# One core, three layers fused: weight conversions split into held steps, and key features and spatial-weight conversions held behind expert work

## The chip, the core and the metric

One core of a Trainium2 chip runs the whole program. Its engines each work through a list of instructions in a fixed order: TensorE does matmuls (PE in the profile, PEld for the loading of its weights), VectorE (DVE), ScalarE (ACT) and GpSimd (POOL) work element by element, and SyncE (SP) issues the DMAs. An engine waits at an instruction until the semaphores that it needs are set, and everything behind it on that engine waits too. The metric is the device time of one execution in microseconds.

## The reference

For a batch of 4 and a sequence of 1088, in single precision:

```
attention  a = S1 k, b = S2 k;  k_p = outer(a, b) per head (64 features);  q_p the same from q
           kv = sum_s k_p v;  z = sum_s k_p;  x = (q_p kv) / (q_p z + 1e-6)
experts    xk = mu_k x + (1 - mu_k) x_prev;  xr = mu_r x + (1 - mu_r) x_prev
           x = sigmoid(xr w_r) * (relu(xk w_k)^2 w_v)            128 -> 1024 -> 128
gMLP       h = relu(x w_in);  u, v = halves of h (512 each);  v_n = v normalised over its 512
           v_s = w_spatial v_n + b_spatial;  out = (u * v_s) w_out     w_spatial: 1088 x 1088
```

## The kernel before, in words

A matmul operand is split into a high part H and a rest L, both in a rounded format, and a product is three matmuls (`mm3`, L126: H by H, H by L, L by H). So every weight and every activation is converted first: a copy into H (`copy`, L129, on ACT) and a subtraction that leaves L (`low`, L132, on DVE or POOL).

The weights of the layers w_k, w_v, w_r, w_in and w_out arrive in 64-bit form. `split64` turns one block of 512 columns into H and L by integer work: on DVE L139, L141, L142, L143 and L144, on ACT L140, L146 and the copy into H, on POOL the product L147. The late ones, two blocks of w_in and one of w_out, are called `conv_late`. The spatial weight arrives in single precision, in 27 tiles (k, c): 9 blocks of rows k, of which the last (k = 8) holds the 64 rows of the tail and the bias, by 3 chunks c of 384, 384 and 320 columns. `wload` fetches a tile into one of two raw buffers (`st`), `wconv` converts it, and `wstep` does both, one tile behind the other. Raw tiles of both kinds go through one list, `pending_raw`, first in, first out.

The time up to some 210 us is one loop over g = 0 to 99. Step g issues the up-projection of one of 96 expert blocks (`up`: matmuls `p<-m,k`, a relu on ACT at L355, a square on POOL at L358 or on DVE at L363), the split of the square (`sqsplit`, L375 or L387 and L132) and the down-projection four steps behind (`down`: `p<-w,xs1H`, `p<-w,wvT`, then the gating on DVE at L403). A table of planned steps (`plan(g, fn)`) adds at each g what else is due:

- `q_feat`, `q_turn`, `q_num`, `q_out` for the next chunk of queries: matmuls L203, features on DVE or POOL (L214, tile `n1L`), transposes L255, products L272, a division on DVE (L276 to L278), and a transpose back, L290, copied to `x`.
- `prep`: on POOL the difference of neighbours (L312, `m<-x`), on DVE the mix (L313, `mx`), then H on ACT and L on DVE (tile `m`): the moving operand of 8 steps of `up`. `prep_r` does the same for the gate (L329, tiles `xrH` and `xrL`, the latter by POOL).
- `k_feat` for batches 2 and 3: three chunks each of key features, into `n0H`, `n0L` and `n1H`. Each is 6 matmuls (L203), a copy on ACT and one product of 768 columns (L214) on DVE, except `n0H` of batch 2 and `n0L` of batch 3, which POOL makes. They are needed by `k_sum`, some steps later.
- `x_tile` and `v_tile` of batch 0 (the v half of h): `p<-winL,w`, `p<-winH,w`.
- the conversions above, and from g = 93 on the first spatial products (`spatial`): `p<-w,n0H` and `p<-w,n0L` for d = 0, `p<-w,n1H` and `p<-w,n1L` for d = 1, each over 8 blocks k, and the tail (L561, L562, tile `T`). After the loop those of d = 2 (`p<-w,m`) and d = 3 (`p<-w,k`) follow.

The order of instructions on each engine isn't the order of this code. A scheduler goes over the traced program with an estimate of times and puts next on an engine what it takes to be ready first, so that an instruction whose operands are early can land far ahead of work that the code issues before it. What limits this is `behind(anchors, fn)`: an instruction that `fn` issues gets an edge to the anchor on its own engine and is not placed ahead of it. `anchor` holds three instructions, the last ones of the expert work so far on DVE, ACT and POOL. `late(fn)` is `behind` with all three. Before the change, `conv_late` is held by the DVE anchor alone and as one piece; `wconv` by the DVE and ACT anchors, and only for chunk c = 0; `k_feat` by nothing.

Of the kernel before, what the change touches and what calls it, by code (L numbers as in the profile page):

```python
# [18 lines left out]
NF = DFF // 128  # L19
# [16 lines left out]
NFILL = 3  # L36
VP = 2 * (HD + 1)
G1 = 26
WS = 30
WR = 2.5  # L40
C0 = 17
CS = 6
# [37 lines left out]
def attn_moe_gmlp(ctx: ExitStack, tc: tile.TileContext, qT, kT, va, st, wk, wv, wr, win, wout,  # L80
# [10 lines left out]
    def sb(tag, shape, dt=F32):  # L91
        uid[0] += 1
        return pool.tile(shape, dt, tag=tag, bufs=1, name=f"{tag}_{uid[0]}")
# [7 lines left out]
    def rot(*tags):  # L101
        i = count.get(tags, 0)
        count[tags] = i + 1
        return tags[i % len(tags)]
# [23 lines left out]
    def copy(dst, src):  # L128
        return SE.activation(out=dst, in_=src, func=AF.Copy)  # L129
# [1 line left out]
    def low(eng, L, src, H):  # L131
        return eng.tensor_tensor(out=L, in0=src, in1=H.bitcast(F32), op=ALU.subtract)  # L132

    def split64(raw, n, H, L, total=None):
        hi, lo = raw[:, :, 1], raw[:, :, 0]
        x = rot(*CVT)
        th, s = sb(f"w{x + 1}", [128, 2, n], I32), sb(f"w{x + 2}", [128, n], I32)
        t, h = th[:, 0], th[:, 1]
        VE.tensor_scalar(out=t, in0=hi, scalar1=0x7FFFFFFF, scalar2=9, op0=ALU.bitwise_and, op1=ALU.logical_shift_right)  # L139
        SE.activation(out=h, in_=t, func=AF.Relu, scale=4096.0, bias=ebias)  # L140
        VE.tensor_scalar(out=s, in0=hi, scalar1=0x1FF, scalar2=15, op0=ALU.bitwise_and, op1=ALU.logical_shift_left)  # L141
        VE.scalar_tensor_tensor(out=s, in0=lo, scalar=17, in1=s, op0=ALU.logical_shift_right, op1=ALU.bitwise_or)  # L142
        VE.scalar_tensor_tensor(out=h, in0=hi, scalar=-0x80000000, in1=h, op0=ALU.bitwise_and, op1=ALU.bitwise_or)  # L143
        VE.tensor_scalar(out=t, in0=h, scalar1=-0x800000, scalar2=None, op0=ALU.bitwise_and)  # L144
        if total is None and n in CONVP:
            SE.activation(out=s.bitcast(F32), in_=s, func=AF.Copy, scale=2.0 ** -35)  # L146
            GE.tensor_tensor(out=L, in0=s.bitcast(F32), in1=t.bitcast(F32), op=ALU.mult)  # L147
        else:
            VE.scalar_tensor_tensor(out=L, in0=s, scalar=2.0 ** -35, in1=t.bitcast(F32), op0=ALU.mult, op1=ALU.mult)
        if total is None:  # L150
            copy(H, h.bitcast(F32))
        else:
            VE.tensor_tensor(out=total, in0=h.bitcast(F32), in1=L, op=ALU.add)

    def flat(r):
        return r.rearrange("p a b -> p (a b)")

    pending_raw = []
# [6 lines left out]
    def conv64():  # L165
        split64(*pending_raw.pop(0))
# [131 lines left out]
    anchor, prep_L = [None, None, None], [None, None]  # L298
# [547 lines left out]
    SE.activation(out=warm, in_=half, func=AF.Sigmoid)  # L846
    Sl, Ss = sb(m(10), [128, 16]), sb(m(8), [128, 16])
    split64(rawS, 16, None, Sl, Ss)
    Sb = sb("Sbd", [128, 2 * NH, 16])
    VE.tensor_tensor(out=Sb, in0=Ss.unsqueeze(1).to_broadcast([128, 2 * NH, 16]),  # L850
# [13 lines left out]
    at = [-1]  # L864
# [3 lines left out]
    def wnext():  # L868
        if wi[0] < len(worder):
            k, c = worder[wi[0]]  # L870
            free = {t: QE[2 + (t > 1)] if t < 4 else GL + GW if t < 8 else C0 + 2 * CS + 1 for t in range(17)}
            if at[0] < max([free.get(t, 0) for t, _ in wplace(k, c)] + [W1G if c == 1 else NI * NF if c else 0]):
                return
            wload(k, c)
        wi[0] += 1

    def wstep():
        if pending_raw:
            behind([x for x in anchor[:2] if x is not None and pending_raw[0][1] == 0], wconv)
        wnext()  # L880

    load_q(0, (0,))
# [14 lines left out]
    def behind(anchors, fn, *a):  # L897
        with ExitStack() as es:
            for x in anchors:
                es.enter_context(tc.issue_after(x.ins))  # L900
            fn(*a)
# [31 lines left out]
    def plan(g, fn, *a):  # L933
        todo.setdefault(g, []).append(lambda: fn(*a))

    def gated(fn):
        return wraps(fn)(lambda *a: behind(prep_0, fn, *a))

    NI = B * NCH
    QS = [None, 0, 4] + [8 + QD * n for n in range(NI - 3)]  # L940
    QS[1:] = [x + y for x, y in zip(QS[1:], QJ[1:])]
    for j in range(1, NI):
        sp = 1 if j < 3 else 2
        for n, fn in enumerate((q_feat, q_turn, q_num, q_out)):
            plan(QS[j] + sp * n, gated(fn) if j < 3 and n == 0 else fn, j)
        e = QS[j] + 3 * sp
        plan(max(8 * j - 6, e + 1), prep, j)
        plan(max(8 * j - 4, e + 2), prep_r, j)
        plan(8 * j - 2, receive, j)
        plan(8 * j - 1, gate, j)  # L950
    QE = [QS[3 * b + 2] + 1 for b in range(B)]
    for b in range(1, B):
        last = QS[3 * b]
        ks = (3, 6, 8) if b == 1 else (last - 19, last - 12, last - 5)
        for c in range(NCH if b > 1 else 0):
            plan(ks[c], k_feat, b, c)
        if b > 1:
            plan(last + 1, k_sum, b, 0)
            plan(last + 2, k_sum, b, 1)
        if b + 1 < B:  # L960
            plan(last + 3, load_v, b + 1)
            plan(QE[b - 1], load_k, b + 1)
            plan(QE[b - 1], load_q, b + 1)
    def late(fn, *a):
        behind([x for x in anchor if x is not None], fn, *a)

    def conv_first():
        late(conv64)

# [1 line left out]
        H, L = [x.bitcast(F32).rearrange("p (f two d) -> p f two d", two=2, d=128)[:, 2 * h:2 * h + 2, 1] for x in (wvH, wvL)]  # L971
        GE.tensor_tensor(out=wvT[:, 2 * h:2 * h + 2], in0=H, in1=L, op=ALU.add)

    def conv_late():
        behind(anchor[:1], conv64)

    for n in range(2):
        plan(R0[n], total_wv, n)
# [3 lines left out]
    plan(R1 + 4, gate, 0)  # L982
    for n, x in enumerate(wseq[5:]):
        plan(C0 - 2 + CS * n, load64, *x)
        plan(C0 + CS * n, conv_late)
    for n in range(2):
        plan(WS - 2 + n, wnext)
    for n in range(NK + 1):
        plan(WS + int(WR * n), wstep)
    xv["v"] = sb("tt", [128, NT - HALF, DG])  # L990
    xv["x"] = sb("w17", [128, 4, 2, 128], F32R)
    for j in range(NT):
        plan(VS[j] - 1, late, x_tile, j)
        plan(VS[j], late, v_tile, 0, j)
        plan(VS[j] + 1, late, v_rest)
# [3 lines left out]
    for n in range(8):  # L999
        plan(GL + GW + n, wstep)  # L1000
# [158 lines left out]
```

## Time and profile before

| what | value |
|---|---|
| three runs | 456.65, 456.32, 456.0 us; median 456.32 |
| the profiled execution | 456.75 us, of which the span from first to last instruction is 455.0 |
| mean granted clock of TensorE | 0.999 of full speed |
| busy, PE / PEld / DVE / ACT / POOL | 445.3 / 422.2 / 293.8 / 264.1 / 221.5 us |
| instructions | 7558 |

Times in the rows below are counted from the first instruction. The loop over g starts at 23 us on TensorE; g = 17 begins at 63 us, g = 34 at 91 us, g = 54 at 121 us, g = 95 at 201 us. Tile names are printed without their buffer numbers, so `m` and `w` stand for many tiles, and a line is often that of a helper. The ends of matmuls are modelled and overlap; the weight load, PEld, has gaps of its own.

### The profile page before, as it was taken

The page shows a single profiled execution, that of the slowest core. Times are in us where ns is not written, and L with a number is a line of the kernel's source. Part 1 is how long each engine was busy: PE and PEld are TensorE (multiplying, and loading weights), DVE is VectorE, ACT ScalarE, POOL GpSimd, SP SyncE. Part 2 cuts the span into 40 slices and gives each one's busy share as a digit, 9 for nine tenths or more (in the row PEclk, how much of TensorE's full clock was granted, in tenths as well). Part 3 has the DMA queues.
Part 4 walks back from the last instruction along what each step waited for, and adds up shares of the span by engine and source line. Part 5 has one row for each costly group of instructions (what it writes and reads, how often), then busy time and mean ns, then how long its engine had stood idle before and what let it go on. Part 6 is the DMA issues. An engine that isn't in the chain of part 4 may idle for free.

```text
span 455.0 us, 7558 instructions
## 1 busy us (share of the span) xinstructions
PE 445.3 (98%) x2697; PEld 422.2 (93%) x2697; DVE 293.8 (65%) x520; ACT 264.1 (58%) x613; POOL 221.5 (49%) x267
## 2 busy tenths in 40 slices
PE   8989999989999999999999999999999999999997
PEld 8977899969998899899999999999999999999996
DVE  4597768879787874446786377882665861634513
ACT  2495878887977886876545454543455433434322
POOL 2558457496757685557223243334434534335220
PEclk9999999999999999999999999999999999999999
DMA  7982100011200031024243732312022222010001
GB/s 209 353 284 93 50 0 2 0 37 35 63 1 1 9 97 53 1 79 127 70 138 134 231 102 100 110 46 71 14 84 71 93 83 84 29 40 24 0 1 49
DMA packets 30949, 34.91 MB, mean 77 GB/s; under 512 B 2816, under 2 KB 26432, under 8 KB 30912
## 3 DMA queue, kind: packets, MB, share of 16 engines
q1 hardware_dynamic: 30912, 34.44, 23.7%
q8 instruction: 21, 0.34, 0.3%
q14 instruction: 16, 0.13, 0.1%
HBM read 25.91 MB, written 8.52 MB: 76 GB/s over the span
## 4 chain that ended last, share of the span: by engine, by line
PE 75%; DVE 9%; DMA 5%; ACT 5%; POOL 3%; issue 2%; SPq 1%; ACTq 0%; DVEq 0%; POOLq 0%
PE p L126 62%; PE p L399 4%; PE p L272 2%; DMA VR<-vd 2%; DMA w<-in_wk_dram 1%; PE p L720 1%; PE p L719 1%; DMA w<-in_qT_dram 1%; PE p L203 1%; DVE mx L313 1%; PE p L234 1%; DVE w L143 1%; ACT m L129 1%; DVE w L142 1%; PE p L255 1%
## 5 line engine op out<-in xcount | busy, mean ns | idle before, releaser
L126 PE MATMUL p<-w,k 128*128 128x384 f32 (+1 forms) x384 | 69.5, 325 | 0.0
L126 PE MATMUL p<-m,k 128*128 128x384 f32 (+1 forms) x288 | 65.6, 349 | 1.4 <-ACT m L129 1.2
L126 PEld LDWEIGHTS p<-w,k 128*128 128x128 f32 x384 | 63.6, 188 | 1.0 <-ACT k L129 0.4
L614 DVE TENSOR_TENSOR m<-p,m 128x384 f32<-128x384 f32 (+2 forms) x37 | 18.7, 518 | 57.2 <-PE p L720 56.4
L126 PEld LDWEIGHTS p<-m,k 128*128 128x128 f32 x288 | 48.4, 188 | 6.4 <-ACT m L129 1.7
L132 POOL TENSOR_TENSOR k<-VR,k 128x512 fp32r<-128x512 f32 x23 | 30.8, 1341 | 38.8 <-ACT k L129 36.0
L355 ACT ACTIVATE m<-p 128x384 f32<-128x384 f32 (+1 forms) x96 | 42.5, 469 | 10.2 <-PE p L126 9.6
L132 DVE TENSOR_TENSOR m<-m,m 128x384 fp32r<-128x384 f32 (+1 forms) x47 | 33.2, 707 | 20.4 <-ACT m L129 16.8
L129 ACT ACTIVATE m<-m 128x384 fp32r<-128x384 f32 (+2 forms) x44 | 22.1, 504 | 38.4 <-DVE m L733 18.4
L126 PE MATMUL p<-w,n1H 128*128 128x384 f32 (+1 forms) x204 | 42.1, 326 | 0.0
L358 POOL TENSOR_TENSOR m<-m 128x384 f32<-128x384 f32 (+1 forms) x35 | 29.8, 859 | 16.3 <-ACT m L355 15.8
L126 PE MATMUL p<-w,n1L 128*128 128x384 f32 (+1 forms) x180 | 36.8, 324 | 0.0
L132 DVE TENSOR_TENSOR w<-m,w 128x384 fp32r<-128x384 f32 (+1 forms) x35 | 26.1, 756 | 14.6 <-POOL m L358 7.6
L126 PEld LDWEIGHTS p<-w,n1H 128*128 128x128 f32 x204 | 34.5, 188 | 0.4
L399 PE MATMUL p<-w,wvT 128*128 128x384 f32 (+1 forms) x88 | 34.3, 471 | 0.0
L129 ACT ACTIVATE m<-p 128x384 f32<-128x384 f32 (+2 forms) x35 | 16.2, 468 | 30.7 <-PE p L126 19.7
L493 POOL TENSOR_SCALAR rs<-mv 128x1 f32<-128x1 f32 x34 | 9.0, 265 | 51.2 <-DVE mv L492 50.4
L126 PEld LDWEIGHTS p<-w,n1L 128*128 128x128 f32 x180 | 30.5, 188 | 0.1
L132 POOL TENSOR_TENSOR n1H<-VR,n1H 128x512 fp32r<-128x512 f32 x11 | 14.2, 1287 | 31.8 <-ACT n1H L129 26.3
L129 ACT ACTIVATE k<-VR 128x512 fp32r<-128x512 f32 x23 | 14.4, 630 | 25.6 <-PE p L126 17.5
L126 PE MATMUL p<-w,xs1H 128*128 128x384 f32 (+1 forms) x88 | 24.8, 337 | 0.4 <-DVE w L132 0.4
L126 PE MATMUL p<-m,woH 128*128 128x384 f32 (+1 forms) x86 | 24.4, 329 | 0.3 <-DVE m L132 0.3
(284 smaller groups left out, 1185.4 us busy)
## 6 DMA issues: line engine op xcount, KB each, us to landing
vd<-VR SPq DMA_DIRECT2D x24, 256.0 KB, 2.0
VR<-vd SPq DMA_DIRECT2D x24, 256.0 KB, 3.0
st<-in_wT_dram SPq DMA_DIRECT2D x16, 192.0 KB, 2.4
VR<-in_wT_dram SPq DMA_DIRECT2D x9, 192.0 KB, 2.7
w<-in_kT_dram SPq DMA_DIRECT2D x8, 192.0 KB, 5.3
w<-in_qT_dram SPq DMA_DIRECT2D x8, 192.0 KB, 4.0
out_dram<-m SPq DMA_DIRECT2D x8, 192.0 KB, 1.9
m<-in_wT_dram SPq DMA_DIRECT2D x7, 192.0 KB, 4.7
```

The costliest lines, as they stand in the source:

```text
L126: TE.matmul(out_ap, lhsT=l, rhs=r, start=first and n == 0, stop=last and n == 2, skip_group_check=skip)
L129: return SE.activation(out=dst, in_=src, func=AF.Copy)
L132: return eng.tensor_tensor(out=L, in0=src, in1=H.bitcast(F32), op=ALU.subtract)
L142: VE.scalar_tensor_tensor(out=s, in0=lo, scalar=17, in1=s, op0=ALU.logical_shift_right, op1=ALU.bitwise_or)
L143: VE.scalar_tensor_tensor(out=h, in0=hi, scalar=-0x80000000, in1=h, op0=ALU.bitwise_and, op1=ALU.bitwise_or)
L203: TE.matmul(wide[:, 64 * t:64 * t + 128], lhsT=src[:, cut(c, t, CH[c][0])], rhs=Sbd, start=True, stop=True)
L272: nd_pe[0] = TE.matmul(o.rearrange("p h c -> p (h c)"), lhsT=qt[g][:, cut(c, t)], rhs=kb[:, g], start=not wide or g == 0, stop=not wide or ...
L355: SE.activation(out=r, in_=hk, func=AF.Relu)
L358: anchor[2] = GE.tensor_tensor(out=sq, in0=r, in1=r, op=ALU.mult)
L399: TE.matmul(vvs[i], lhsT=wvT[:, f // 2], rhs=hls.pop(g), start=f == 0, stop=f == NF - 1)
L493: GE.tensor_scalar(out=rs, in0=mv[:, 1:2], scalar1=1e-6, scalar2=None, op0=ALU.add)
L614: return eng.tensor_tensor(out=o, in0=a, in1=b_, op=op)
```

## The change

```
-WS = 30
+WS = 34

-def split64(raw, n, H, L, total=None):
+def split64_steps(raw, n, H, L, total=None):
     ...                       # tiles, then: yield
     L139, L140 (ACT)          # yield
     L141                      # yield
     L142                      # yield
     L143                      # yield
     L144, L146 (ACT), L147 (POOL), copy into H (ACT)      # yield
+def split64(*a):
+    for _ in split64_steps(*a):
+        pass

 def wstep():
     if pending_raw:
-        behind([x for x in anchor[:2] if x is not None and pending_raw[0][1] == 0], wconv)
+        behind([x for x in anchor if x is not None and at[0] < NI * NF], wconv)

-    plan(ks[c], k_feat, b, c)
+    plan(ks[c], late, k_feat, b, c)

-def conv_late():
-    behind(anchor[:1], conv64)
+steps = []
+def conv_begin():
+    steps.append(split64_steps(*pending_raw.pop(0)))
+    conv_step()
+def conv_step(last=False):
+    late(next, steps[-1])
+    if last:
+        next(steps.pop(), None)

     plan(C0 - 2 + CS * n, load64, *x)
-    plan(C0 + CS * n, conv_late)
+    plan(C0 + CS * n, conv_begin)
+    for i in range(1, CS - 1):
+        plan(C0 + CS * n + i, conv_step, i == CS - 2)
```

(The lines of `split64` are shown here by their numbers in the kernel before.) The three late 64-bit conversions, planned as one piece at g = 17, 23 and 29, become five pieces each, at g + 1 to g + 4; all but the last piece are held behind all three anchors of their step. The key features of batches 2 and 3 keep their steps (9, 16, 23 and 33, 40, 47) and are held. The conversions of the spatial weight are held behind all three anchors while g < 96, for every chunk, and those of chunk 0 are planned from g = 34 on instead of 30. The numbers of instructions and of DMAs stay.

How this moves instructions, at three places on POOL. The first is some 40 us into the program: `n0H<-sab` is a key feature of batch 2, `n1L<-sab` a query feature, `m<-x` and `xrL` belong to `prep` and `prep_r`, and `w<-m,w` to the expert blocks. Before:

```order
L312 TENSOR_TENSOR m_114_436<-x_60_238 128x384
L214 TENSOR_TENSOR n0H_565<-sab_570 128x768
L214 TENSOR_TENSOR n1L_711<-sab_716 128x768
L132 TENSOR_TENSOR xrL_457<-mx_454,xrH_456 128x384
L132 TENSOR_TENSOR w_146_536<-m_138_509,w_146_536 128x384
L132 TENSOR_TENSOR xrL_474<-mx_471,xrH_473 128x384
L312 TENSOR_TENSOR m_173_637<-x_60_238 128x320
```

After:

```order
L322 TENSOR_TENSOR m_114_436<-x_60_238 128x384
L132 TENSOR_TENSOR xrL_457<-mx_454,xrH_456 128x384
L132 TENSOR_TENSOR w_146_536<-m_138_509,w_146_536 128x384
L224 TENSOR_TENSOR n0H_565<-sab_570 128x768
L132 TENSOR_TENSOR xrL_474<-mx_471,xrH_473 128x384
L132 TENSOR_TENSOR w_165_606<-m_159_579,w_165_606 128x384
L224 TENSOR_TENSOR n1L_711<-sab_716 128x768
L322 TENSOR_TENSOR m_173_637<-x_60_238 128x320
```

Both features now stand behind the gate's `xrL`, one and two expert pieces later.

The second place is at about g = 34: `woL` is the POOL part of the last 64-bit conversion, `w<-st` are conversions of the spatial weight, `n0L<-sab` is a key feature of batch 3, `m<-m` an expert square and the last row the difference for the next `prep`. Before:

```order
L147 TENSOR_TENSOR woL_87<-w_295_1044,w_294_1043 128x512
L132 TENSOR_TENSOR w_317_1134<-st_304_1092,w_317_1134 128x384
L214 TENSOR_TENSOR n0L_1324<-sab_1329 128x768
L358 TENSOR_TENSOR m_327_1165<-m_326_1163 128x384
L132 TENSOR_TENSOR w_342_1210<-st_318_1137,w_342_1210 128x384
L312 TENSOR_TENSOR m_329_1172<-x_195_704 128x320
```

After:

```order
L368 TENSOR_TENSOR m_312_1108<-m_311_1106 128x384
L368 TENSOR_TENSOR m_326_1162<-m_325_1160 128x384
L322 TENSOR_TENSOR m_328_1169<-x_195_704 128x320
L132 TENSOR_TENSOR w_334_1184<-st_316_1127,w_334_1184 128x384
L152 TENSOR_TENSOR woL_87<-w_295_1044,w_294_1043 128x512
L368 TENSOR_TENSOR m_345_1219<-m_344_1217 128x384
L132 TENSOR_TENSOR w_354_1241<-st_323_1152,w_354_1241 128x384
```

The difference for `prep` has passed `woL`, both conversions and the key feature, which comes seven rows behind the last row shown.

The third place is the end of the expert loop: `w<-st` of 384 columns are the blocks k = 5, 6 and 8 of chunk 1, and the rows from `m<-tt` on are the split of the normalised v for d = 2 (`m`) and d = 3 (`k`). Before:

```order
L132 TENSOR_TENSOR w_731_2458<-st_726_2445,w_731_2458 128x384
L132 TENSOR_TENSOR w_742_2514<-st_732_2461,w_742_2514 128x384
L358 TENSOR_TENSOR m_715_2412<-m_714_2410 128x320
L132 TENSOR_TENSOR w_757_2582<-st_749_2533,w_757_2582 128x384
L358 TENSOR_TENSOR m_723_2437<-m_722_2435 128x320
L132 TENSOR_TENSOR w_342_1210<-st_759_2589,w_317_1134 128x320
L358 TENSOR_TENSOR m_740_2507<-m_739_2505 128x320
L132 TENSOR_TENSOR m_780_2705<-tt_341,m_779_2704 128x256
```

After:

```order
L368 TENSOR_TENSOR m_740_2507<-m_739_2505 128x320
L132 TENSOR_TENSOR w_742_2514<-st_732_2461,w_742_2514 128x384
L132 TENSOR_TENSOR m_780_2705<-tt_341,m_779_2704 128x256
L132 TENSOR_TENSOR k_783_2713<-VR_63,k_782_2712 128x512
L132 TENSOR_TENSOR k_783_2713<-tt_341,k_782_2712 128x512
L132 TENSOR_TENSOR m_778_2699<-VR_63,m_777_2698 128x128
L132 TENSOR_TENSOR m_778_2699<-tt_341,m_777_2698 128x256
L1043 COPY wvT_2722<-tt_341 128x512
L132 TENSOR_TENSOR m_776_2695<-VR_63,m_775_2694 128x384
L132 TENSOR_TENSOR w_757_2582<-st_749_2533,w_757_2582 128x384
```

The block k = 8 of chunk 1, `w_757`, stood ahead of the last two squares and now stands behind the last square, one conversion and the seven rows that prepare d = 2 and 3.

## Rows read from the trace of the kernel before

**Rows 1.** The page, first part: busy us (share), and instructions.
```profile
PE 445.3 (98%) x2697; PEld 422.2 (93%) x2697; DVE 293.8 (65%) x520; ACT 264.1 (58%) x613; POOL 221.5 (49%) x267
```
**Rows 2.** Busy time by stretch: start:end, length, engines, clock, DMA share, GB/s.
```profile
88.00:104.00 16.00, 14.62 (x74) 11.65 (x73) 12.98 (x18) 13.66 (x36) 13.89 (x15) 1.00 0.14 38
```
**Rows 3.** Waits of PE, 40 to 104 us: total us, times, longest.
```profile
PE p L126 <- ACT m L129: 1.2, 2, 0.6
PE p L126 <- DVE w L132: 0.4, 1, 0.4
PE p L272 <- ACT x L129: 0.3, 1, 0.3
PE p L126 <- ACT w L129: 0.3, 1, 0.3
```
**Rows 4.** Waits of the weight load, PEld, 40 to 104 us.
```profile
PEld p L126 <- ACT m L129: 1.7, 2, 0.9
PEld p L126 <- DVE w L132: 0.9, 1, 0.9
PEld p L272 <- ACT x L129: 0.6, 1, 0.6
PEld p L126 <- ACT w L129: 0.5, 1, 0.5
PEld p L126 <- DVE m L132: 0.4, 1, 0.4
```
**Rows 5.** The chain that ended last, 40 to 56 us: start, us, what.
```profile
41.40 1.86 DVE mx L313
...
44.43 1.76 DVE mx L329
```
**Rows 6.** Timeline of POOL, 40 to 60 us: start, us, instruction, idle before.
```profile
41.33 1.51 POOL L214 TENSOR_TENSOR n0H<-sab 128x768 f32<-128x768 f32 x1
44.10 1.67 POOL L214 TENSOR_TENSOR n1L<-sab 128x768 f32<-128x768 f32 x1 [1.27 <-ACT sab L129]
```
**Rows 7.** Timeline of DVE: the same two operations later.
```profile
48.26 0.61 DVE L329 SCALAR_TENSOR_TENSOR mx<-m,mus,x 128x384 f32<-128x384 f32 x1
...
80.74 0.62 DVE L313 SCALAR_TENSOR_TENSOR mx<-m,mus,x 128x384 f32<-128x384 f32 x1 [0.72 <-POOL m L312]
```
**Rows 8.** Timeline of ACT at 92 us: the copy of a chunk of x.
```profile
92.25 0.52 ACT L129 ACTIVATE x<-p 128x384 f32<-128x384 f32 x1
```
**Rows 9.** Timeline of POOL, 91 to 98 us.
```profile
91.84 1.34 POOL L132 TENSOR_TENSOR w<-st,w 128x384 fp32r<-128x384 f32 x1
93.14 1.56 POOL L214 TENSOR_TENSOR n0L<-sab 128x768 f32<-128x768 f32 x1
...
95.45 1.02 POOL L132 TENSOR_TENSOR w<-st,w 128x384 fp32r<-128x384 f32 x1
96.43 1.03 POOL L312 TENSOR_TENSOR m<-x 128x320 f32<-128x320 f32 x1
```
**Rows 10.** Waits of the weight load, PEld, 104 to 250 us.
```profile
PEld p L126 <- ACT m L355: 0.4, 1, 0.4
...
PEld p L126 <- POOL m L132: 0.3, 1, 0.3
```
**Rows 11.** Timeline of POOL, 185 to 222 us.
```profile
197.37 1.01 POOL L132 TENSOR_TENSOR w<-st,w 128x384 fp32r<-128x384 f32 x1 [1.93 <-ACT w L129]
...
203.93 0.98 POOL L132 TENSOR_TENSOR m<-tt,m 128x256 fp32r<-128x256 f32 x1
...
213.91 0.94 POOL L1023 COPY wvT<-tt 128x512 f32<-128x512 f32 x1
```
**Rows 12.** Timeline of PE, 192 to 212 us: the first tail product of chunk 1.
```profile
202.72 0.34 PE L561 MATMUL p<-w,T 128*128 128x384 f32 x1
```
**Rows 13.** The chain that ended last, later: start, us, matmuls.
```profile
275.77 12.76 PE p L126 x72
```
**Rows 14.** Timeline of PE at 263 us.
```profile
263.35 0.41 PE L126 MATMUL p<-m,woH 128*128 128x320 f32 x1 [0.31 <-DVE m L132]
```

More of the change, by code (lines that the diff above doesn't have):

```diff
@@ L138, in split64 @@
         t, h = th[:, 0], th[:, 1]
+        yield
         VE.tensor_scalar(out=t, in0=hi, scalar1=0x7FFFFFFF, scalar2=9, op0=ALU.bitwise_and, op1=ALU.logical_shift_right)
         SE.activation(out=h, in_=t, func=AF.Relu, scale=4096.0, bias=ebias)
+        yield
         VE.tensor_scalar(out=s, in0=hi, scalar1=0x1FF, scalar2=15, op0=ALU.bitwise_and, op1=ALU.logical_shift_left)
+        yield
         VE.scalar_tensor_tensor(out=s, in0=lo, scalar=17, in1=s, op0=ALU.logical_shift_right, op1=ALU.bitwise_or)
+        yield
         VE.scalar_tensor_tensor(out=h, in0=hi, scalar=-0x80000000, in1=h, op0=ALU.bitwise_and, op1=ALU.bitwise_or)
+        yield
         VE.tensor_scalar(out=t, in0=h, scalar1=-0x800000, scalar2=None, op0=ALU.bitwise_and)
@@ L153, in split64 @@
             VE.tensor_tensor(out=total, in0=h.bitcast(F32), in1=L, op=ALU.add)
+        yield
+    def split64(*a):
+        for _ in split64_steps(*a):
+            pass
     def flat(r):
@@ L950, in attn_moe_gmlp, with late @@
         plan(8 * j - 1, gate, j)
+    def late(fn, *a):
+        behind([x for x in anchor if x is not None], fn, *a)
     QE = [QS[3 * b + 2] + 1 for b in range(B)]
@@ L963, in attn_moe_gmlp @@
             plan(QE[b - 1], load_q, b + 1)
-    def late(fn, *a):
-        behind([x for x in anchor if x is not None], fn, *a)
     def conv_first():
```

## The prediction

> **What bounds the kernel now.** I read the page first. PE is busy for 98% of the span, so whatever is gained must come out of the few places at which PE waits, and everything else is about who makes it wait [rows 1]. The reader is to see in that row that DVE, ACT and POOL have room on the average. The average hides the stages, so the busy time by stretches came next: from 88 to 104 us POOL works for 13.89 of 16 us, and the weight load falls to 11.65 of 16 [rows 2]. There POOL, not PE, sets the pace.
>
> Then the waits of PE and of its weight load, from 40 us (no engine's order changes before that) to 104 us. PE's own rows name four waits of 2.2 us in total, 1.2 + 0.4 + 0.3 + 0.3 [rows 3]. The weight load, which must have its operand before a matmul can start, names the same ones and one more, with 4.1 us, 1.7 + 0.9 + 0.6 + 0.5 + 0.4 [rows 4]. A matmul in flight covers a part of a weight load's wait, and PE's modelled ends cover more than there is, so the loss lies between the two: 2.2 to 4.1 us. From 104 to 250 us the weight load's waits are small [rows 10].
>
> A page of the Trainium skill bears on which of the two to take: Trainium Kernel Development and Optimization, section Best Practices, tells one to judge TensorE by its weight-load share and not by its matmul share. By it the 4.1 us would count in full and the forecast be 0.8 us lower than below (0.6 in the first term, 0.2 in the second); the page row has 98% and 93%, which agrees that the two differ [rows 1].
>
> Last the chain of waits, and POOL's and DVE's timelines beside it. At 41.40 us DVE's mix for the next chunk (`mx`, L313) takes 1.86 us, and at 44.43 the gate's mix (L329) 1.76 us [rows 5]. The same operations take 0.62 and 0.61 us elsewhere [rows 7]. Beside the two long ones POOL runs a feature product, from 41.33 for 1.51 us and from 44.10 for 1.67 us [rows 6]. So a POOL feature beside a DVE mix costs the mix about 1.2 us, and the mix leads by way of ACT's H to the next `up`: the first of the two waits for ACT's `m` [rows 3, 4].
>
> The second lies at 99 us. The chunk of x that its `prep` needs was copied from 92.25 to 92.77 us [rows 8]. POOL takes the difference (L312) at 96.43 us only, because a spatial-weight conversion, a key feature of 1.56 us and another conversion stand ahead of it [rows 9]. All three were put there early by the scheduler; nothing needs them soon.
>
> **The change, part by part.** No instruction and no DMA is added or removed. The three 64-bit conversions keep their five DVE, three ACT and one POOL instructions each, a spatial tile its copy, its subtraction and its load on SP. What changes is who stands in front of whom, so each term is a wait that goes or comes, not a duration.
>
> *Key features held.* At 41 us POOL's two features now stand behind the two `xrL`. Both mixes should run alone: 1.86 - 0.62 = 1.24 us and 1.76 - 0.61 = 1.15 us sooner. That is more than the wait of the weight load there (0.9 us, the longest of two in [rows 4]), so this wait goes in full, and PE is next limited by its own list, which has the same work in it. DVE's own features of batch 2 leave this place too, so the wait for ACT's `x` (0.3 to 0.6 us) goes with it. At 92 us the difference has passed `woL`, the conversions and the feature. It can start at 92.8 instead of 96.4, 3.6 us sooner; the other wait for ACT's `m` and the one for DVE's `m` (0.4 us in rows 4 alone) go. Together, by PE's rows 1.2 + 0.3 = 1.5 us, by the weight load's 1.7 + 0.6 + 0.4 = 2.7 us; I take the middle, 2.1.
>
> *Conversions in held steps and later.* What is left at 100 to 102 us are the waits for ACT's `w` (the x tile of `v_tile`) and DVE's `w` (an expert's L): 0.7 us by PE, 1.4 by the weight load [rows 3, 4]. The conversions come later and one step at a time, but POOL's 13.89 us in this stretch [rows 2] only thin out to the next one. I take half of the middle, 0.5 us. That the conversions end four steps later costs nothing: w_in is needed by `v_tile` at g = 34 and done at 27, w_out and chunk 0 by the spatial products at g = 93 and done at 54. On SP the loads of chunk 0 keep their places in its list; further on four loads for batch 1 pass those of chunk 2, whose conversions come later anyway.
>
> *What the moved features meet.* Six features of batches 2 and 3 must run somewhere: two on POOL, four on DVE. Each could again make a mix 1.2 us longer. At the lowest they meet nothing urgent and cost 0, at the highest both POOL features cost 1.2 us each. The nearest rows are the later stretch, in which the same kind of work runs and single waits are 0.4 us [rows 10]; I take one of these, 0.4.
>
> *Chunk 1 of the spatial weight.* Now its conversions are held behind the last expert steps. On POOL its tail, at 197.37 us before [rows 11], stands behind the last square and seven operations that prepare d = 2 and 3, which take from 203.93 to 214.85 us [rows 11]. PE used that tail at 202.72 us [rows 12]. So the product d = 0, chunk 1 can't end then, nor the next one, and PE's order now has d = 3 and d = 2 ahead of them: two products of 24 matmuls, at 12.76 / 72 = 0.177 us each [rows 13], 8.5 us to fill the gap. If that suffices the cost is 0. If PE must stand for one product of 24, it is 4.25 us. The waits in this stage were 0.4 and 0.3 us [rows 10], and I take their sum, 0.7.
>
> *The hand-over to batches 1 to 3* has one wait of 0.3 us [rows 14]. The orders there change a little; I count nothing, and 0.3 either way.
>
> The sum, against the profiled execution of 456.75 us (its span of 455.0 and 1.75 around it): 456.75 - 2.1 - 0.5 + 0.4 + 0.7 = 455.25 us. The median of the runs is 456.32, 0.43 lower than that execution; so a run should take 454.8 us.
>
> **The rivals.**
>
> *The collisions come again.* POOL's list is as long as before. For it: DVE and POOL are both busy for over four fifths of the stretch from 88 to 104 us [rows 2]; a feature of 1.5 us lands beside something. Against it: the later a feature is, the less depends on it. With both POOL features at 1.2 us each: 456.32 - 2.1 - 0.5 + 2.4 + 0.7 = 456.8 us, no change within the noise or nearly so. A rule of the Trainium skill speaks for this rival and so against the change: SBUF — State Buffer, section Who interferes with whom, says that a DVE instruction with two SBUF inputs and a GpSimd one that reads SBUF exclude each other for the whole instruction, whichever starts first. By that rule holding a feature moves the block of 1.2 us to its next neighbour and removes none; the trace agrees on the block itself, 1.86 against 0.62 us [rows 5, 7].
>
> *PE starves for chunk 1* (slower). The place is 200 to 216 us, the point from which it decides is that POOL's tail conversion with the small copy, DMA and copy that follow it ends after PE has used up the 8.5 us of d = 2 and 3. For it: POOL's seven operations alone need 10.9 us in the trace, with their own waits and one conversion. Against it: PE had 4.3 us in hand before (tail done at 198.4, used at 202.72 [rows 11, 12]). With one product's length: 456.32 - 2.6 + 0.4 + 4.25 = 458.4 us.
>
> *More goes than I count.* All of the 4.1 us of [rows 4] and the 0.3 of [rows 14], and nothing comes: 456.32 - 4.4 = 451.9 us; with half of what lies between, 453.3.
>
> **How the numbers follow.** My forecast, 454.8 us, has a chance of 0.50, with 453.6 to 455.7 as its own range. More than that goes: 0.12. The collisions come again: 0.21. PE starves: 0.17. 0.2% of 456.32 is 0.9 us, about what a measurement of this kernel can tell from no change. Faster than 455.4 are the larger gain and most of the forecast: 0.12 + 0.43 = 0.55. Within 0.9 us of the median are the rest of the forecast and nearly all of the second case: 0.07 + 0.19 = 0.26. Slower are the starved case and the rest: 0.17 + 0.02 = 0.19. The range of 8 in 10 goes down to 452.8, half-way into the larger gain, and up to 457.6, where it holds the second case and the milder part of the starved one.
>
> **What would show it.** Right: at about 41 to 45 us both mixes take some 0.6 us; PE has no wait for ACT's `m` in the first 100 us; L312 for the sixth chunk starts within 1 us of its copy of x; PE's waits from 40 to 104 us sum to less than 1 us; from 104 us on the two traces keep their distance. Wrong: a mix of over 1 us beside `n0H` or `n0L` at their new places, with a wait of PE behind it; a gap of PE between 200 and 216 us whose releaser is a `w` tile or the tail `T`; a gap at the first product of batch 1.

## The result, and the profile after

The changed kernel took 459.66 us, the median of six runs (459.07 to 460.13), and the kernel before 456.49 beside it: a ratio of 1.0065, 95% interval 1.0051 to 1.0078. The change made it slower by some 3 us; 454.8 was predicted, and 457.6 was the range's upper end. One execution of g1 below (546.5 us, mean granted clock 0.75) and one of j2 (626.77 us, 0.66) ran at a lower clock than all others and are left out, so that the medians are 461.34 us for g1 and 455.77 us for j2. The profiled execution took 459.95 us, its span 458.2. The page's busy line, to hold against [rows 1]:

```profile
PE 446.0 (97%) x2697; PEld 421.8 (92%) x2697; DVE 282.6 (62%) x520; ACT 264.2 (58%) x613; POOL 219.3 (48%) x267
```

The busy times are those of before within some 2 us, but for DVE's, which fell by 11: 82 of its instructions take over 1.25 times the short durations of their form (the 20th percentile over all runs), against 100 before, and all but 1 and 3 of these overlap one of POOL. PE's busy time grew by 0.7 us and its span by 3.2, so most of the extra time is waiting. The waits of PE from 40 to 104 us (total us, times, longest), which answer to [rows 3]:

```profile
PE p L300 <- DVE VR L288: 1.2, 1, 1.2
PE p L126 <- DVE m L373: 0.7, 1, 0.7
```

All four waits of before are gone, and two new ones of nearly the same sum stand in their place. From 104 us to the end, where before had a single 0.3 us [rows 14]:

```profile
PE p L126 <- DVE x L413: 1.1, 1, 1.1
PE p L126 <- DVE xs0L L132: 0.7, 1, 0.7
PE p L126 <- DVE m L132: 0.7, 2, 0.5
PE p L126 <- ACT m L129: 0.6, 1, 0.6
PE p L282 <- DVE kb L249: 0.2, 1, 0.2
```

A list of waits doesn't say when time is lost for good. For that I gave each matmul its length without waits (0.174 us for 384 columns), summed along PE's timeline of each trace, and took how much later a kernel has done the same work as the kernel before. Each row is set to 0 at 30 us, which takes out differences in the start. Some records are missing, so single entries are good to about 0.2 us. From 44 to 104 us the orders on PE differ most, and there the entries also depend on the length given to the short matmuls: by up to some 1 us at 52, 76 and 92 us. Where both kernels have issued just the same matmuls that length drops out: the changed kernel is 0.1 us ahead at 106 us, and 1.1 us behind at 110, 2.1 at 260 and 3.9 at 268. The rows below the first are the experiments of the next section.

```
us later than before, at   44    52    76    92   104   108   140   148   204   212   260   268 us
the changed kernel       -0.5   0.5   1.5   2.2  -0.4   1.1   1.6   1.9   1.9   2.4   2.1   3.9
e1  features held        -0.5   0.5   1.6   2.1  -0.5  -0.4   1.5   3.0   3.9   4.5   4.2   4.3
e2  steps, g = 34         0.0   0.0   0.1   0.3   1.5   1.5   2.6   5.6   6.2   6.0   5.8   5.4
e3  spatial hold          0.0   0.0   0.0   0.0   0.0   0.1   0.1   0.1   0.2   0.7   0.4   1.4
e4  after, chunk 1 free  -0.5   0.5   1.6   2.3  -0.4   1.1   2.0   3.8   3.7   3.7   3.4   3.3
e7  after, last 4 free   -0.6   0.5   1.5   2.2  -0.4   1.0   1.5   1.8   1.8   2.4   2.1   1.6
g1b product held         -0.7  -0.4   1.4   1.9  -0.7  -0.5   1.1   2.6   3.5   4.4   4.1   4.1
i3  POOL's features      -0.5   0.5   0.4   1.0  -0.1   0.7   1.1   0.9   1.2   1.0   0.8   0.7
j1  DVE's features        0.0   0.1   3.9   4.4   1.8   1.9   4.2   3.6   3.1   3.0   2.8   2.3
h1  g = 34                0.0   0.0   0.1   0.1  -1.4  -1.5   0.9   0.8   0.3   0.3   0.0  -0.6
h2  steps                 0.0   0.0   0.1   0.2   1.7   1.7   2.4   3.3   3.9   4.1   3.8   4.3
i1  g = 34, xs0 held      0.0   0.0   0.0   0.3  -1.5  -1.5  -0.8  -0.8  -1.3  -1.3  -1.6  -2.1
i4  features, xs0 held   -0.5   0.5   1.6   2.1  -0.5  -0.4   0.2  -0.2   1.7   2.2   1.9   1.7
```

In the first row time is lost at 44 to 52 us (1.0), 52 to 92 (1.7), 104 to 108 (1.5), 108 to 148 (0.8) and 260 to 268 (1.8), and won back at 92 to 104 (2.6). All but the 0.8 were then looked up in the trace.

**44 to 52 us.** DVE's timeline of the changed kernel shows both mixes short, as predicted (0.62 us, against 1.86 and 1.76 in [rows 5]):

```profile
40.75 0.62 DVE L323 SCALAR_TENSOR_TENSOR mx<-m,mus,x 128x384 f32<-128x384 f32 x1
...
42.55 0.62 DVE L339 SCALAR_TENSOR_TENSOR mx<-m,mus,x 128x384 f32<-128x384 f32 x1
```

ACT's timeline behind it (start, us, instruction, idle before):

```profile
46.62 0.32 ACT L129 ACTIVATE sab<-p 128x192 f32<-128x192 f32 x1
46.83 0.49 ACT L365 ACTIVATE m<-p 128x384 f32<-128x384 f32 x1
47.20 0.53 ACT L129 ACTIVATE xrH<-mx 128x384 fp32r<-128x384 f32 x1
47.62 0.50 ACT L129 ACTIVATE x<-p 128x384 f32<-128x384 f32 x1
47.99 0.51 ACT L365 ACTIVATE m<-p 128x384 f32<-128x384 f32 x1
```

The feature's copy `sab` was held too. Before it ran at 43.71 us between a copy of `mx` and one of `x`, with 1.86 us of idle time soon after; now it stands in a burst, ahead of two relus (L365). DVE's square (L373) waits for the second of them, and PE for the square:

```profile
49.14 0.80 PE L126 MATMUL p<-m,k 128*128 128x384 f32 x3 [0.74 <-DVE m L373]
```

**52 to 92 us.** PE's longest wait of the first list lies here. DVE and PE of the changed kernel:

```profile
73.41 1.38 DVE L145 SCALAR_TENSOR_TENSOR w<-w,w 128x512 int32<-128x512 int32 x1
...
74.96 0.56 DVE L288 TENSOR_TENSOR VR<-p,de 128x384 f32<-128x384 f32 x1
```
```profile
75.67 0.52 PE L300 MATMUL p<-idn,VR 128*128 128x128 f32 x3 [1.15 <-DVE VR L288]
```

A piece of the second 64-bit conversion (L145, 1.38 us) stands on DVE inside the division of the queries, between its denominator `de` (L286, at 73.30) and the division (L288) for which PE's transposes wait. That is 1.15 of the 1.7 us. The steps alone aren't the reason, though: e1 below, which has none, loses as much in this stretch.

**104 to 108 us.** A line each of POOL, DVE and PE:

```profile
104.62 1.51 POOL L224 TENSOR_TENSOR n0L<-sab 128x768 f32<-128x768 f32 x1
```
```profile
104.70 1.78 DVE L132 TENSOR_TENSOR w<-m,w 128x320 fp32r<-128x320 f32 x1 [1.59 <-POOL m L368]
106.40 0.55 DVE L413 TENSOR_TENSOR x<-p,m 128x384 f32<-128x384 f32 x1
```
```profile
107.00 0.41 PE L126 MATMUL p<-w,xs1L 128*128 128x320 f32 x1 [1.05 <-DVE x L413]
```

The key feature `n0L`, held from 93.14 us [rows 9] to 104.62, lies beside an expert's L, which takes 1.78 us in place of some 0.5; the gating comes late, and PE waits 1.05 us for it. In e1, with all features held too, this place costs nothing (-0.5 to -0.4), in i3, with POOL's alone, 0.8: whether the two meet depends on the rest of the order.

**246 to 268 us, the hand-over.** ACT and then DVE:

```profile
251.38 0.63 ACT L129 ACTIVATE n1H<-VR 128x512 fp32r<-128x512 f32 x1 [3.03 <-DMA VR<-vd]
252.04 0.64 ACT L129 ACTIVATE T<-wvT 64x128 fp32r<-64x128 f32 x2
252.71 0.44 ACT L563 ACTIVATE m<-p 128x320 f32<-128x320 f32 x1
253.17 0.47 ACT L129 ACTIVATE m<-m 128x320 fp32r<-128x320 f32 x1
...
262.07 0.63 ACT L129 ACTIVATE k<-VR 128x512 fp32r<-128x512 f32 x1 [3.86 <-DMA VR<-vd]
```
```profile
253.67 0.49 DVE L132 TENSOR_TENSOR m<-m,m 128x320 fp32r<-128x320 f32 x1 [3.23 <-ACT m L129]
254.08 0.55 DVE L624 TENSOR_TENSOR VR<-VR 128x384 f32<-128x384 f32 x1
254.55 1.15 DVE L507 TENSOR_SCALAR VR<-VR,mv,rs 128x512 f32<-128x512 f32 x2
...
264.63 1.09 DVE L132 TENSOR_TENSOR m<-m,m 128x320 fp32r<-128x320 f32 x1 [4.60 <-ACT m L129]
```

ACT stands for 3.03 us at the first copy of v for batch 1 (`n1H`), whose operand a DMA still brings. Behind it in ACT's list is the copy of a gated output, DVE waits for that, and behind DVE's wait are the last two normalisations of batch 1 (L507), at 254.55 us. In the kernel before they came at 243.51 and 246.41. The writes and loads of v that need them come later too. ACT's second long wait, at 262 us, isn't new, the kernel before has it as well:

```profile
259.62 1.16 ACT L129 ACTIVATE k<-VR 128x512 fp32r<-128x512 f32 x2 [3.90 <-DMA VR<-vd]
```

What is new is what comes behind it: `n1L`, copied at 252.35 us before, is now copied at 263.13, between the wait and the next gated output. PE waits three times (0.6 + 0.2 + 0.7 us) from 264.6 to 268.1. The start of it all: the first matmul of batch 1's `v_tile` runs at 227.0 us, before at 212.8 (in e3 below at 226.2, in e7 at 215.4).

### The profile page after: what moved, and what is told of

Same layout as the page of the kernel before. It is cut to its first block, busy times and chain, and to the rows that moved or that the text cites. A ratio compares the mean times of both kernels' runs of the same rounds, so it can differ in the third digit from the quotient of the medians.

```text
span 458.2 us, 7538 instructions
## 1 busy us (share of the span) xinstructions
PE 446.0 (97%) x2697; PEld 421.8 (92%) x2697; DVE 282.6 (62%) x520; ACT 264.2 (58%) x613; POOL 219.3 (48%) x267
## 4 chain that ended last, share of the span: by engine, by line
PE 81%; DVE 9%; ACT 4%; DMA 2%; POOL 2%; issue 2%; SPq 0%; ACTq 0%; DVEq 0%; POOLq 0%
PE p L126 63%; PE p L409 5%; PE p L213 3%; PE p L282 3%; DMA VR<-vd 2%; PE p L244 2%; PE p L730 1%; PE p L729 1%; PE p L265 1%; DVE xs0L L132 1%; DVE w L132 1%; PE p L853 1%; DVE w L145 1%; ACT m L365 1%; PE p L300 1%
## 5 line engine op out<-in xcount | busy, mean ns | idle before, releaser
L126 PE MATMUL p<-m,k 128*128 128x384 f32 (+1 forms) x288 | 66.6, 347 | 1.1 <-DVE m L373 0.7
L365 ACT ACTIVATE m<-p 128x384 f32<-128x384 f32 (+1 forms) x96 | 43.5, 469 | 14.7 <-PE p L126 13.7
L507 DVE TENSOR_SCALAR VR<-VR,mv,rs 128x512 f32<-128x512 f32 x24 | 19.7, 826 | 8.0 <-POOL rs L504 7.9
```

The source lines that it names most:

```text
L126: TE.matmul(out_ap, lhsT=l, rhs=r, start=first and n == 0, stop=last and n == 2, skip_group_check=skip)
L365: SE.activation(out=r, in_=hk, func=AF.Relu)
L507: VE.tensor_scalar(out=v, in0=r, scalar1=mv[:, 0:1], scalar2=rs, op0=ALU.subtract, op1=ALU.mult)
```

## The experiments

Fourteen runs; g1b is the kernel of g1 once more, for a trace at the full clock. Names as in the table. "Before" and "after" are the kernel before and the changed one.

**e1, e2, e3: one part of the change each, on top of before.**

```
e1  plan(ks[c], late, k_feat, b, c)
e2  WS = 34; conv_begin / conv_step in place of conv_late
e3  behind([x for x in anchor if x is not None and at[0] < NI * NF], wconv)
```

> The kernel before with one part of the change: the key features of batches 2 and 3 held. Theory (each loss belongs to one part: the hand-over to the hold on chunk 1, the wait at 75 us to the conversion steps): both mixes at 41 to 45 us take 0.6 us, the wait for ACT's m at 43 us is gone, no new wait at 49, 75 or 265 us; 456.5 - 1.2 to - 2.0, so 454.5 to 455.3 us. Rival (any new order shifts waits about, and the loss belongs to no part): within 0.9 us of 456.5, with new waits at other places that eat the gain.

> The kernel before with one part of the change: the three late 64-bit conversions in five held steps, and the conversions of chunk 0 planned from g = 34 on. Theory: the q_out transposes near 75 us wait for the query's division as in the changed kernel (1.1 us), because pieces of the second conversion stand ahead of it on DVE; the waits for the w tiles at 100 to 102 us are gone (0.7 us); the hand-over is as before; 456.5 + 1.1 - 0.7 = 456.9 us, 456.2 to 457.6. Rival: the wait at 75 us is absent, since the held key features caused it; 455.8 us.

> The kernel before with one part of the change: every conversion of the spatial weight in the expert loop held behind the DVE, ACT and POOL anchors. Theory: the first v tile of batch 1 starts on PE at about 226 us instead of 213, the last two normalisations of it come at about 254 us instead of 243 to 246, and PE loses 1.8 us between 246 and 268 us and 0.6 at 205; 456.5 + 2.4 = 458.9 us, 458.2 to 459.5. Rival: the hand-over stays as before, and only the 0.6 us at 205 us is lost; 457.1 us.

Measured: e1 461.31 us (ratio 1.011, 1.0092 to 1.0129), e2 462.31 (1.0134, 1.0119 to 1.0149), e3 459.33 (1.0068, 1.0042 to 1.0094), against 456.28. Each part alone makes the kernel slower. (At a mean clock of 0.998 to 1.000 e1 took 460.31 and 460.69 us and e3 458.09 and 458.38, at 0.995 1.2 to 2.4 us more; the rows in the table are from the former.) e1 and e2 fell out against the theory in size and place. e1 has the gain at 41 and 99 us and the loss at 44 to 52, but also the loss at 52 to 92 that I had put down to the steps; e2 hasn't got that one. By 104 us e1 is 0.5 us ahead: what it has lost at the end, 4.3 us, it loses from 108 us on, with PE waiting 1.55 us at 142.73 for the mask `kb` and 0.82 at 169.83 for a normalised v tile. e2 loses 1.2 us from 92 to 104 and 3.0 from 140 to 148, with waits of 1.07 us at 93.91 for an x tile, 1.03 at 145.83 for the mask and 1.55 at 151.85 for a query division. The parts don't add up either: 4.3 + 5.4 + 1.4 = 11.1 us by the last column, and together 3.9.

e3 went as its theory said in place: till 204 us its row is 0, and then ACT and DVE show the hand-over of the changed kernel again, with the first v tile at 226.2 us and the last two normalisations at 253.53. In size it is less: 0.5 us at 204 to 212 and 1.0 at 260 to 268, where 0.6 and 1.8 were expected.

```profile
250.36 0.64 ACT L129 ACTIVATE n1H<-VR 128x512 fp32r<-128x512 f32 x1 [2.89 <-DMA VR<-vd]
...
260.46 0.63 ACT L129 ACTIVATE k<-VR 128x512 fp32r<-128x512 f32 x1 [3.28 <-DMA VR<-vd]
```
```profile
253.53 1.14 DVE L497 TENSOR_SCALAR VR<-VR,mv,rs 128x512 f32<-128x512 f32 x2
```

**e4, e7: the hold on chunk 1 taken back, in after.**

```
e4  behind([x for x in anchor if x is not None and pending_raw[0][1] == 0], wconv)
e7  behind([x for x in anchor if x is not None and at[0] < GL], wconv)        # GL = 88
```

> The changed kernel with the hold on chunk 1 of the spatial weight taken back (chunk 0 stays held behind all three anchors). Theory: the v tiles of batch 1 and the quad loads stand where they stood before, the losses at 205 and at 246 to 268 us go; 459.7 - 2.4 = 457.3 us, 456.6 to 457.8. Rival (the hand-over loss comes with the whole order): 459.0 to 459.7 us.

> The changed kernel with the hold of the spatial conversions ended at g = 88, so that chunk 0 and the first five tiles of chunk 1 stay held and the last four, whose buffers come free at g = 92, do not. Theory: the losses of 0.5 us at 205 to 212 us and 1.0 to 1.8 us at 260 to 268 us go, and the wait for the mask kb at 144 us (1.8 us when all of chunk 1 was free) does not come; 459.7 - 2.0 = 457.7 us, 457.2 to 458.3. Rival (the hand-over depends on the whole of chunk 1): 459.2 to 460 us.

Measured: e4 460.61 us (1.011, 1.0083 to 1.0136, against 456.28), e7 458.73 (1.0034, 1.0019 to 1.0048, against 456.89). In both the hand-over loss of 1.8 us is gone (last two columns: -0.1 and -0.5 in place of +1.8). Both times lie above what was expected, e7's by 0.4 us: it still loses 0.6 us at 204 to 212, which e4 doesn't. In e7 ACT waits as little at these two copies as before:

```profile
250.25 0.63 ACT L129 ACTIVATE n1H<-VR 128x512 fp32r<-128x512 f32 x1 [0.72 <-PE p L126]
...
254.95 0.63 ACT L129 ACTIVATE n1L<-VR 128x512 fp32r<-128x512 f32 x1 [1.05 <-DMA VR<-vd]
```

So it was the hold on the last four tiles of chunk 1 that cost the hand-over: e7 takes away these alone, e4 the hold on the whole chunk, and e3, which adds the hold on all tiles, brings 1.0 of the 1.8 us. e4 lost 1.8 us elsewhere, at 140 to 148 us, and so missed its number: PE waits 1.75 us for the key-value mask `kb` of batch 3, which DVE runs behind the four subtractions of `xs0`. In after PE comes to the mask when it is nearly done (0.2 us).

**g1 and g1b, i3, j1: which half of a key feature costs.**

```
g1  before; only L214 of k_feat behind the anchors, POOL's sab in a buffer of its own
i3  before; late, k_feat   for (b, c) = (2, 0) and (3, 1) alone, which POOL makes
j1  before; late, k_feat   for the four others, which DVE makes
```

> The kernel before with only the product of a key feature (L214 on POOL or DVE) held; its six matmuls, its copy on ACT and the query features stand free as before, and the POOL feature gets a buffer of its own in place of sab. Theory A (holding the whole feature lost because its matmuls, PE's filler at 40 to 49 us, and the next query feature went with it): PE has no wait for DVE's m at 48 us, the mix at 41 us takes 0.6 us, and the lateness against the kernel before at 52 us is 0.5 to 1 us lower than with the whole feature held; 455.3 to 456.3 us. Theory B (POOL's and DVE's products are what matters, wherever they go they meet something): 458 us or more, with waits of 1 us at new places between 44 and 100 us.

> The same kernel as the one with only the product of a key feature held, for a profile at the full clock. Theory A (the whole feature's loss at 44 to 52 us came from its copies on ACT and its matmuls on PE, which moved with it): by 52 us it has lost nothing against the kernel before, where the whole feature held had lost 0.5 us, and no wait for DVE's m at 48 us. Theory B (the products alone are what matters): it has lost 0.4 us or more by 52 us. Its time, 460 to 462 us, is known; the trace is to show where from 52 us on it is lost.

> The kernel before with only the two key features that POOL makes held (n0H of batch 2, n0L of batch 3); the four on DVE stay free. Theory (the gains at 42 and 99 us came from POOL's features, the losses at 48 and 74 us from the copies and query features behind the first one): the waits for ACT's m at 43 and 99 us go (1.7 by the weight load), the loss at 44 to 52 us stays (1.0), so 455.8 to 456.6 us. Rival (the losses came from DVE's features): 455.0 us or less.

> The kernel before with only the four key features that DVE makes held; POOL's two stay free. Theory (DVE's features, held into the stretch of the query division, delay it): a loss of about 1.2 us between 68 and 76 us, none between 44 and 52, and the mixes at 41 and 44 us take 1.8 us as before; the waits at 98 to 102 us largely stay; 457.5 to 459.5 us. Rival (the loss needs POOL's features as well): no loss at 68 to 76 us; 456 to 457 us.

Measured: g1 461.34 us (1.0087, 1.0056 to 1.0119), g1b 461.01 (1.0098, 1.0075 to 1.0122), i3 457.32 (1.0013, 1.0002 to 1.0024), j1 458.82 (1.006, 1.004 to 1.008). g1b has lost nothing by 52 us (-0.4 where e1 has +0.5) and has no wait for DVE's `m`: the loss at 44 to 52 us did come from the copies and matmuls that moved with the product; which of the two weighs more, and what the buffer of its own for POOL's `sab` did, wasn't separated. In this g1's theory A holds, but its time is missed by 5 us. g1b loses 1.8 us from 52 to 76 instead and has won it back by 104 (-0.7). The 4.1 us at its end are lost after 108, as in e1, with PE waiting 1.54 us for the mask at 143.45 and 0.79 for a v tile at 170.44. i3 has the loss at 44 to 52 us and nothing at 52 to 76; j1 the reverse, so the second belongs to DVE's features. i3's time lies 0.7 us above what was expected, and the loss at 74 us that its theory put down to POOL's feature isn't there. j1's expectation had the place, but not the size (3.8 us, of which the last section takes 1.7 out). i3, with a bit of the gain and of the loss, is the mildest form of the hold, and still not faster (PE waits 0.72 us at 95.27 and 0.57 at 107.74, at new places).

**h1, h2: the conversions apart from each other.**

```
h1  before; WS = 34
h2  before; conv_begin / conv_step in place of conv_late, WS = 30
```

> The kernel before with one number changed: conversions of chunk 0 planned from g = 34 on instead of 30, nothing held that was not. Theory: they leave the stretch of 91 to 100 us, in which POOL was busy for 13.89 of 16 us, and the waits at 98 to 102 us shrink by half; 455.5 us, 455.0 to 456.0. Rival (what comes later meets x_tile, v_tile and the next prep): the wait moves on, 456.3 to 458 us.

> The kernel before with the three late 64-bit conversions in five held steps and nothing else (chunk 0 still from g = 30 on). Theory: a step held behind the expert work comes back on DVE in front of the relu's square and the gating, so the wait of 1.2 us at 92 us that the same edit had with chunk 0 from g = 34 stays, and those at 144 and 150 us too; 460 to 462 us. Rival: those waits came from chunk 0 moved into 100 to 150 us; 456.5 to 458 us.

Measured: h1 456.69 us (0.9994, 0.9979 to 1.001), as its rival said, and h2 460.88 (1.0076, 1.0049 to 1.0103), as its theory said, against 456.89. The steps alone cost 4 us. ACT and PE of h2 at 93 us:

```profile
93.29 0.63 ACT L151 ACTIVATE w<-w 128x512 f32<-128x512 int32 x1 [1.88 <-DVE w L145]
93.83 0.51 ACT L397 ACTIVATE w<-m 128x384 fp32r<-128x384 f32 x1
94.24 0.29 ACT L129 ACTIVATE w<-x 128x128 fp32r<-128x128 f32 x1
```
```profile
94.58 0.50 PE L126 MATMUL p<-winL,w 128*128 128x512 f32 x1 [1.89 <-ACT w L129]
```

The conversion's copy on ACT (L151) waits 1.88 us for the step on DVE that feeds it (L145, at 92.06), which now comes late; behind it in ACT's list stand an expert's H and the x tile for which PE waits. Moving chunk 0 from g = 30 to 34 alone does what the whole change was predicted to do at 98 to 104 us (-1.5), and loses it by 140 us: 0.57 for a relu behind a copy on ACT that waits for a DMA, and 0.73 for the mask. DVE and PE of h1:

```profile
137.16 2.87 DVE L132 TENSOR_TENSOR xs0L<-x,xs0H 128x384 fp32r<-128x384 f32 x4
139.96 0.28 DVE L239 TENSOR_TENSOR kb<-p,mk 128x132 f32<-128x132 f32 x1
```
```profile
140.29 1.55 PE L272 MATMUL p<-kb,VR 128*128 128x66 f32 x12 [0.73 <-DVE kb L239]
```

**i1, i4, j2: the mask freed.** Nothing needs `xs0` before g = 93, so its split is held at g = 76.

```
-    plan(V0, xsplit, 0)
+    plan(V0, late, xsplit, 0)          i4: with e1's edit;  i1: with WS = 34;
                                        j2: as i1, and wconv held as in e7
```

> The kernel before with chunk 0 planned from g = 34 on, and with the split of the final x of batches 0 and 1 (tile xs0) held behind the expert work of its step, g = 76, so that its four subtractions no longer stand on DVE ahead of the key-value mask kb. Theory: the gain of 1.4 us at 98 to 104 us stays, the wait for kb (0.7 us) at 140 us goes; 456.5 - 1.4 + 0 to 0.6 = 455.1 to 455.7 us. Rival (the four subtractions meet something else later): 456.2 us or more.

> The kernel before with all key features of batches 2 and 3 held, and the split of xs0 held at g = 76. Theory: of the loss of the features alone (4.3 us in the trace), the wait for kb at 141 us (1.5 to 1.7 us) goes and the rest stays; 461.3 - 1.6 = 459.7 us, 459 to 460.2. Rival: the place at 141 us is not bound by the mask, and the time stays at 461 us.

> The faster version (chunk 0 from g = 34 on, split of xs0 held) with the conversions of the spatial weight held behind all three anchors until g = 88, which leaves the last four tiles of chunk 1 free. Theory (the hold cost only by the hand-over, and chunk 0 and the first five tiles of chunk 1 keep their places): the same time within 0.6 us, 454.2 to 455.4 us. Rival (a held conversion meets expert work): 455.8 us or more.

Measured: i1 454.81 us (0.9964, 0.995 to 0.9978), i4 458.40 (1.0036, 1.002 to 1.0051), both against 456.56; j2 455.77 (0.999, 0.9977 to 1.0003, against 456.25). i1 is faster than both kernels, and by 0.3 us more than expected; the held split alone, with chunk 0 still from g = 30, wasn't run. In its DVE timeline the mask comes first and the four subtractions 30 us later:

```profile
137.10 0.28 DVE L239 TENSOR_TENSOR kb<-p,mk 128x132 f32<-128x132 f32 x1
...
167.14 3.64 DVE L132 TENSOR_TENSOR xs0L<-x,xs0H 128x384 fp32r<-128x384 f32 x4
```

i4 shows the same on e1: from 140 to 148 us it loses nothing where e1 lost 1.5. It is 2.9 us faster than e1 (some 2.1 against e1's two runs at the full clock), where 1.6 were expected, and so falls below its range; the table has 1.3 us before 140 us, ahead of the mask, which the mask doesn't explain. j2 lies between its theory and its rival, 0.03 us from the rival's bound: the hold, even without the last four tiles, gives up most of what i1 had won. One place shows in its trace, the slowest of its nine executions: PE waits 0.85 us at 101.73 us, where i1 waits 0.20, for the L of an x tile that takes DVE 1.09 us in place of 0.28 beside a spatial conversion on POOL.

## Why the prediction was wrong, point by point

*Key features held (-2.1).* **The first step that failed.** It said that the waits for ACT's `m` and `x` and for DVE's `m` go, and that PE is next limited by its own list. The first half holds: all of them went. The second doesn't. I had counted the feature's product on POOL and DVE, and not its copy on ACT and its six matmuls on PE, which the same edit moves; the order that I quoted showed POOL alone. The copies moved into a burst of ACT and cost 1.0 us at 44 to 52 (e1, i3; gone in g1b), DVE's features cost 1.1 at 52 to 76 (e1; more in j1, not in i3). By 104 us the changed kernel is 0.4 us ahead, where I had 2.2.

I also misread [rows 8]. The copy of x at 92.25 us has 384 columns and is the seventh chunk's; the sixth has 320, and its copy ran long before, so that it wasn't what would let the difference start at 92.8 us. The copy of the kernel before, and POOL of the changed one:

```profile
70.38 0.44 ACT L129 ACTIVATE x<-p 128x320 f32<-128x320 f32 x1
```
```profile
93.75 0.83 POOL L322 TENSOR_TENSOR m<-x 128x320 f32<-128x320 f32 x1 [1.61 <-DVE x L413]
```

In the changed kernel the difference starts as a gating on DVE ends (93.68 us), and 4.6 us ahead of the seventh chunk's copy (98.33). That it came within 1 us of the time I gave is luck; that it left the conversions and the feature behind is right.

*Conversions in held steps (-0.5).* That POOL sets the pace from 88 to 104 us was read too strongly: [rows 2] has PE busy for 14.62 of the 16 us and POOL for 13.89. The waits at 98 to 102 us did go, but not through the steps: planning chunk 0 later does that alone but for 0.12 us (h1), holding the features alone does it too (e1 has no wait of PE from 74 to 113 us), and the steps alone make it worse (h2, +1.7 at 104). What I wrote, that they end four steps later at no cost, looked at who needs the result, and not at ACT's instructions that wait within the list for a DVE step held back.

*What the moved features meet (+0.4).* Right mechanism, too small a size: one collision of 1.2 us, at 104 us, with a wait of 1.05 of PE behind it, and 1.5 us in the table. This was the first rival, with the price that I had given it for one feature. But the rival as a whole came to 456.8 us, and the collision makes up only a part of the miss. That a DVE instruction with two SBUF inputs contends with a GpSimd one that reads SBUF, as the Trainium skill has it (SBUF — State Buffer, section Who interferes with whom), is what this row shows too: 1.78 us beside a POOL instruction of 1.51.

*Chunk 1 (+0.7).* Right in size, 0.5 us at 204 to 212 us in after and in e3, but not by the mechanism, so partly luck. PE waits neither for a `w` tile nor for `T`, but for an expert's L, which takes DVE 1.48 us in place of 0.49 beside the preparation of d = 3 on POOL. DVE and PE of the changed kernel:

```profile
204.57 1.48 DVE L132 TENSOR_TENSOR m<-m,m 128x320 fp32r<-128x320 f32 x1 [3.38 <-ACT m L397]
```
```profile
206.11 0.42 PE L126 MATMUL p<-m,xs1H 128*128 128x320 f32 x1 [0.47 <-DVE m L132]
```

The rival in which PE starves for chunk 1 didn't come about.

*The hand-over (0, "0.3 either way").* **The second step that failed**, and the largest single loss that isn't won back: 1.8 us. I saw that chunk 1's conversions would be later and asked only whether PE would need them; the raw buffers pass on to chunk 2 (its last conversion ran at 231.7 us, before at 219.9), the products that use it and `v_tile` of batch 1 are ordered after that, and v goes through DRAM and back before ACT may copy it. e3 shows 1.0 us of it alone, e4 and e7 the changed kernel without it.

*The sum.* I added terms of three edits. The rows e1, e2, e3 and after show that such a sum doesn't exist here: 11.1 us apart, 3.9 together. It also had no term for 108 to 148 us, where the changed kernel loses 0.8. The order on every engine is made anew by the scheduler, and the same edit is worth something else in another order.

Of what was to show it, the short mixes and the missing waits for ACT's `m` came true, and L322 for the sixth chunk runs at 93.75 in place of 96.43 us [rows 9], though not within 1 us of its copy of x. Untrue: PE's waits from 40 to 104 us sum to 1.9 and not below 1, and the two traces don't keep their distance after 104 us.

Still open: why e1 loses at 52 to 92 us and g1b at 52 to 76, what the changed kernel loses at 108 to 148, and what j2 loses besides the 0.85 us; they were not traced to an instruction.

## What to carry to other kernels

A hold moves every instruction of what it holds, on every engine: look at the copy on ACT and the matmuls on PE as well as at the long product. Ask of an instruction that is held or made late not only who needs its result, but who stands behind the next instruction that waits for it: an engine at a wait is lost to its whole list, as ACT for 3.03 us at a copy that waited for a DMA. And where a scheduler makes the order, try each edit alone before summing; one number (chunk 0 four steps later) and one held split together brought 1.7 us, the whole change cost 3.

## What the runs showed of the hardware

A long wait of PE can be followed by a stretch at the lower clock, and then costs more than its length. In j1 PE waits 1.75 us for DVE's `m`. Busy time by stretch (start:end, length, PE, PEld, DVE, ACT, POOL, granted clock, DMA share, GB/s), and PE at this place:

```profile
70.00:72.00 2.00, 0.41 (x2) 0.42 (x3) 2.00 (x3) 0.37 (x2) 1.12 (x2) 1.00 0.00 0
72.00:74.00 2.00, 2.00 (x17) 1.81 (x16) 2.00 (x4) 1.94 (x5) 0.47 (x1) 0.90 0.00 0
74.00:77.00 3.00, 3.00 (x9) 2.41 (x8) 2.10 (x6) 1.32 (x3) 2.60 (x3) 0.50 0.00 0
77.00:78.00 1.00, 1.00 (x9) 1.00 (x9) 1.00 (x3) 0.00 (x0) 0.79 (x2) 1.00 0.00 0
```
```profile
71.59 0.62 PE L126 MATMUL p<-m,k 128*128 128x384 f32 x2 [1.75 <-DVE m L132]
```

Two microseconds after the wait, with PE busy again, the clock is 0.50 (1.2 of 2.4 GHz) from 74 to 77 us and 0.90 in the stretch before: (1 - 0.50) x 3 + (1 - 0.90) x 2 = 1.7 us lost. It doesn't follow every such wait. e4 has one of the same length, 1.75 us, and its clock stays at 1.00:

```profile
144.00:146.00 2.00, 0.34 (x2) 0.00 (x0) 2.00 (x3) 1.94 (x6) 2.00 (x3) 1.00 0.00 0
146.00:152.00 6.00, 5.90 (x39) 5.47 (x40) 3.46 (x9) 4.07 (x11) 3.80 (x4) 1.00 0.00 1
```

Nor does h2's clock fall after its wait of 1.89 us, and j1's other execution had a mean clock of 1.000 and took 458.36 us, 0.9 less. So the wait alone doesn't decide it, and what does is open. Executions of one kernel spread by about as much: h1's ten are six of 455.83 to 456.91 us at a mean clock of 0.999 or 1.000, and four of 457.16 to 457.77 at 0.995 or 0.996. That a wait like j1's stands behind the four isn't shown, since no trace of them was kept.
